# Zero fills of a decode kernel: DRAM as the source of zeros for the feed-forward stage and the end

## The chip, the cores and the metric

The kernel runs on one core of one Trainium2 chip. The metric is the device time of one execution in microseconds. The core has four computing engines, TensorE (PE), VectorE (DVE), ScalarE (ACT) and GpSimd (POOL), and SyncE (SP), which here only issues DMA transfers. All transfers, from whichever engine they are issued, run on the core's 16 DMA engines.

## The reference

The reference is the forward and backward pass of one decoder layer with adaptive layer norm, for a single token. It returns the output row and the gradients of ten inputs:

```python
mod = (silu(c) @ w_mod).reshape(1, 6, 1, 1024)      # sa, ca, ga, sb, cb, gb
h = layernorm(x) * (1 + ca) + sa
x = x + ga * attention(h, k_cache, v_cache, wq, wo)  # 32 heads, 4 KV heads, last 4096 of 65536 rows
h = layernorm(x) * (1 + cb) + sb
x = x + gb * ((sigmoid(h @ w_gate) * (h @ w_up)) @ w_down)   # 1024 -> 3584 -> 1024
out, vjp = jax.vjp(f, A_x, k_cache, v_cache, wq, wo, w_gate, w_up, w_down, c, w_mod)
return (out, *vjp(grad_out))
```

The attention reads only the last W = 4096 rows of each cache. The gradients of the two caches have the full shape [1, 4, 65536, 128], however, and all rows ahead of the last 4096 are zero. So 61,440 rows of 256 bytes are to be written with zeros for each of four KV heads and two caches: eight regions of 15 MB, 120 MB in all. (1 MB in this document's counts of fills is 1,048,576 bytes; the profile's MB are 1,000,000.)

## The kernel before, in words

**Stages.** The kernel loads the weights of the modulation, K and V, and wq (to about 50 us), computes scores and softmax, then for each KV head a product N of K, P and V (line 657), the fold of wo into the attention's gradient (`bch`, line 712, 64 steps), the modulation's remaining sections, the feed-forward stage in seven blocks of 512 columns (about 315 to 485 us), and an end in which the gradients of wo, w_mod, wq, K and V are formed and stored. The order of all work is written out by hand; the tile framework adds the waits between engines, and the schedule is not reordered.

**Fills.** The 120 MB of zeros are cut into 120 pieces of 1 MB. `zero(n, after)` issues the next n of them from POOL's queue; tables (`Z_Q`, `Z_SM`, `Z_N`, `Z_B`, `Z_GA`, `Z_CB`, `Z_FOLD`, `Z_FFN`, `Z_END`) say how many at each point of the program. `after` makes the fill wait for an earlier instruction, for pacing. A fill is one of three kinds:

- *Narrow* (7 pieces at positions 15, 45, 75, 93, 103, 113, 119 of the order): columns of the first region, as two DMAs (lines 173 and 176), 120 rows and a small remainder, from an SBUF tile `zeros`. The other rows' remainder is written once by `zero_rest`.
- *From SBUF* (line 186, 44 pieces): the tile `zeros` holds 128 partitions of 2048 one-byte zeros, and the DMA widens them to four bytes, so that each partition writes 8 KB. All fills outside the N and `bch` loops are of this kind, and those pieces of the first region that come up in them.
- *From DRAM* (line 180, 69 pieces): with `big=True`, which only the N loop and `bch` pass, the source is the first quarter of `zero_src`, a piece that has already been filled with zeros, widened in the same way. 32 rows of 32 KB are written.

```python
zero(Z_N[s], recent(mm, 6), True)       # N loop
zero(Z_B[nbq - 1 - len(bq)], recent(mm, 3), True)   # bch
zero(Z_GA)                              # all others: no third argument
```

The order of the pieces is `zero_src`, the eight wide pieces of the first region (128 rows at a stride of 122,880 bytes, 8 KB each), then the other seven regions, which are contiguous, with the narrow ones put in at their positions.

**Queues.** POOL's queue carries the fills, the loads of w_gate and w_up (`load_ug`, line 886, 512 KB each), the stores of their gradients (`store_ug`, line 890), and the stores of the end (lines 1164, 1169, 1205, 1212, 1216). POOL has eight DMA semaphores, used in turn, so that a DMA on it waits until the one eight before has landed. SP's queue carries w_down: `load_wd` (line 872) and `store_wd` (line 875), two halves of 512 KB for each block, in one buffer, so that the load of a half waits for the store of the same half. In each block VectorE's products with w_down (`wd_ttr`, line 227, and `wd_outer`, line 223) come after the matmuls `ffn_mm` (line 999), which wait for the load.

In each block q, `Z_FFN[q]` gives the fills at four places: after the first `store_ug`, after the second, after the last `wd_outer`, and after the second `load_ug` of block q + 2.

Of the kernel before, what the change touches and what calls it, by code (L numbers as in the profile page):

```python
# [10 lines left out]
P = 128  # L11
FP32 = mybir.dt.float32
BF16 = mybir.dt.bfloat16
FP8 = mybir.dt.float8e4
# [11 lines left out]
G = 4  # L26
# [11 lines left out]
NARROW = (15, 45, 75, 93, 103, 113, 119)  # L38

def spread(total, n):
    return [(i + 1) * total // n - i * total // n for i in range(n)]

NBP = 8
NT = 8
NGA = 9
# [5 lines left out]
Z_N = spread(31, 128)  # L53
Z_B = [n + (i in (31, 38)) for i, n in enumerate(spread(29, 43))] + [1, 1, 1, 1, 0] + [1, 0, 0, 1, 1, 1, 0, 0] + [1, 0, 1, 0, 1, 0, 0, 0]
# [4 lines left out]
def kernel(  # L59
# [26 lines left out]
    nc = tc.nc  # L86
    SKW = A_k_cache.shape[2] - W
# [16 lines left out]
    def vt(shape, name, dt=FP32):  # L104
        return pool.tile(shape, dt, name=name)
# [4 lines left out]
    ZW = 4096  # L110
    zeros = vt([P, ZW // 2], "zeros", FP8)
# [11 lines left out]
    def fill_rows(og, g):  # L123
        return og[0, g, 0:SKW, :].rearrange("r d -> (r d)")

    first_rows = fill_rows(out_2, 0).rearrange("(p x) -> p x", p=P)
    NZR = first_rows.shape[1] // ZW
    zregions = [first_rows[:, i * ZW:(i + 1) * ZW] for i in range(NZR)]
    flat = []
    for og in (out_2, out_3):  # L130
        for g in range(G):
            if og is not out_2 or g:
                whole = fill_rows(og, g).rearrange("(i x) -> i x", i=NZR)
                flat.extend(whole[i:i + 1, :] for i in range(NZR))

    zero_src = flat.pop(0)
    BIGP = 32

    def as_rows(piece, n):
        return piece.rearrange("i (p x) -> (i p) x", p=n)  # L140

    wide = [as_rows(zero_src, P)] + zregions[len(NARROW):] + flat
    narrow = zregions[0:len(NARROW)]
    zleft = []
    while narrow or wide:
        if narrow and (len(zleft) in NARROW or not wide):
            zleft.append((narrow.pop(0), True))
        else:
            zleft.append((wide.pop(0), False))
    nlen = len(NARROW)  # L150
    ncount = list(range(1, nlen + 1))
    NS = SKIP + 1
    rest = out_2[0, 0, 0:SKW, :].rearrange("r d -> (r d)").rearrange("(p x) -> p x", p=P)[0:8, 0:nlen * ZW].bitcast(FP32)
    assert nlen * 2 <= 20

    keep = [0]

    def dep(later, earlier):
        tc.add_manual_dep(later.ins, earlier.ins.name,
# [1 line left out]
                          reason="pace")  # L161

    def zero(n, after=None, big=False):
        for _ in range(n):
            if len(zleft) <= keep[0]:
                return
            region, narrow_ = zleft.pop(0)
            first = None
            if narrow_:  # L170
                nc.gpsimd.inc_swdge_sem([], [], mode="reset_dge_cursor")
                n = nlen - ncount.pop()
                first = nc.gpsimd.dma_start(
                    out=rest[0:NS, 0:nlen * 128].rearrange("p (t x) -> p t x", t=2)[:, :, n * 64:(n + 1) * 64],
                    in_=zeros[0:NS, 0:64].rearrange("p (t x) -> p t x", t=1).broadcast_to([NS, 2, 64]))
                ins = nc.gpsimd.dma_start(
                    out=region[8:P, :].bitcast(FP32).rearrange("(t p) x -> p t x", t=2),
                    in_=zeros[0:60, :].rearrange("p (t x) -> p t x", t=1).broadcast_to([60, 2, ZW // 2]))
            elif big and region.shape[0] == 1:
                ins = nc.gpsimd.dma_start(  # L180
                    out=as_rows(region, BIGP).bitcast(FP32),
                    in_=zero_src[:, 0:P * ZW // 4].rearrange("i (p x) -> (i p) x", p=BIGP).bitcast(FP8))
            else:
                if region.shape[0] == 1:
                    region = as_rows(region, P)
                ins = nc.gpsimd.dma_start(out=region.bitcast(FP32), in_=zeros[:, :])  # L186
            if after is not None:
                dep(first or ins, after)

# [19 lines left out]
    def tt(out, a, b, op):  # L209
        return nc.vector.tensor_tensor(out=out, in0=a, in1=b, op=op)  # L210
# [215 lines left out]
    for j in range(KD):  # L426
        for k in range(16):
            mm = nc.tensor.matmul(mod_ps[:, k:k + 1], lhsT=wm01_t[j][:, k * P:(k + 1) * P],
                                  rhs=cs_bf[:, j:j + 1], start=(j == 0 and k == 0), stop=(j == KD - 1),
                                  skip_group_check=True)  # L430
# [53 lines left out]
    for j in range(KD):  # L484
# [6 lines left out]
        for h in range(HQ):  # L491
            mm = nc.tensor.matmul(q_ps[:, h:h + 1], lhsT=wq_t[j][:, h * P:(h + 1) * P],  # L492
                                  rhs=h1_bf[:, j:j + 1], start=(j == 0 and h == 0), stop=(j == KD - 1),
                                  skip_group_check=True)
# [9 lines left out]
    for ch in range(8):  # L504
        ps = new_ps("sc_ps")
        for g in range(G):
            mm = nc.tensor.matmul(ps[32 * g:32 * g + 32, 0:512], lhsT=q_col2[:, HG * g:HG * g + 32],
                                  rhs=k_T[:, g, ch * 512:(ch + 1) * 512], start=True, stop=True,
                                  tile_position=(0, 32 * g))
# [132 lines left out]
    def recent(mm, lag):  # L642
        last_mm.append(mm)
        return last_mm[-lag] if len(last_mm) >= lag else last_mm[0]

    for g in range(G):
        nbank = bank_pair("n_ps", g)
        for t_ in range(KT):
            s = g * KT + t_
            vp = vp_t[(s // 2) % 2]  # L650
            if t_ % 2 == 0:
                tt(vp.rearrange("p t h d -> p (t h d)"),
                   v_nat[:, g, t_ * DH:(t_ + 2) * DH].rearrange("p (t o d) -> p t o d", t=2, o=1).broadcast_to([P, 2, HG, DH]),
                   pT2[:, g, HG * t_:HG * t_ + 2 * HG, :].rearrange("p n (o k) -> p n o k", o=1).broadcast_to([P, 2 * HG, 64, 2]),
                   ALU.mult)
            for k in range(2):
                mm = nc.tensor.matmul(nbank[k][:, :], lhsT=k_nat[:, g, t_ * DH:(t_ + 1) * DH],  # L657
                                      rhs=vp[:, t_ % 2, 4 * k:4 * k + 4, :].rearrange("p h d -> p (h d)"),
                                      start=(t_ == 0), stop=False)
            zero(Z_N[s], recent(mm, 6), True)  # L660
            if t_ == 20:
                build_bd(g)
            if s == 2:
                ok_cols(ok4)
            elif s == 4:
                ok_rows()
            elif s == 24:
                mod_gb((6, 7))
                load_wo(0)
            elif t_ % 2 == 1:  # L670
                side()
        for k in range(2):
            nc.tensor.matmul(nbank[k][:, :], lhsT=nkb_rows[:, :], rhs=bd[:, 4 * k:4 * k + 4, :].rearrange("p h d -> p (h d)"),
                             start=False, stop=True)
            c0 = (HG * g + 4 * k) * P
            nc.scalar.activation(out=N_sb[:, c0:c0 + 512], in_=nbank[k][:, :], func=ACT.Copy, scale=float(SCALE))
        load_wo(4 + g)
        if g < 3:
            jobs.extend(t_unit(h, "AA") for h in range(HG * g, HG * g + HG))
# [5 lines left out]
    bq = []  # L685
# [13 lines left out]
    nbq = len(bq)  # L699
    bbank = {}  # L700

    def bch(n=1):
        for _ in range(n):
            if not bq:
                return
            p, i, u = bq.pop(0)
            if i == 0:
                bbank[p] = bank_pair("b_ps", p)
            for a in range(4):
                h = 4 * u + a  # L710
                for k in range(2):
                    mm = nc.tensor.matmul(bbank[p][k][:, :], lhsT=a4[:, p, h, :], rhs=wo_t[u][:, a, k * 512:(k + 1) * 512],  # L712
                                          start=(i == 0 and a == 0), stop=(i == 7 and a == 3))
            zero(Z_B[nbq - 1 - len(bq)], recent(mm, 3), True)
            if i == 7:
                for k in range(2):
                    o = B_t[p][:, k * 512:(k + 1) * 512]
                    if k == 0 or p == NBP - 1:
                        nc.scalar.copy(out=o, in_=bbank[p][k][:, :])
                    else:  # L720
                        cp(o, bbank[p][k][:, :])
# [418 lines left out]
    dh1_ps = new_acc("dh1_ps")  # L1140
    for p in range(NBP):
        for it in range(KD):
# [95 lines left out]
    dh1 = vt([P, KD], "dh1")  # L1238
    cp(dh1[:, 0:NBP], dh1_ps[:, 0:NBP])
    dwo(4)  # L1240
# [34 lines left out]
    dx0b, _ = layernorm_bwd_col(dln1, ln1, rstd1, "ln1b")  # L1275
# [58 lines left out]
    for g in (2, 3):  # L1334
# [1 line left out]
        dwq_tile(4 + g, tail)  # L1336
        s2(2 * g, tail)
        s2(2 * g + 1, tail)
    keep[0] = 0
    zero(len(zleft))  # L1340
    assert not zleft and not narrow and not jobs and not bq

# [28 lines left out]
```

## Time and profile before

| What | Value |
|---|---|
| Median of 3 runs | 595.29 us (595.26 to 595.35) |
| The profiled execution's own time | 595.61 us |
| Its span in the profile | 593.8 us |
| Busy share of PE, DVE, ACT, POOL | 68%, 60%, 44%, 26% |
| DMA | 246.61 MB in 36,321 packets, mean 415 GB/s |
| Issues of fills: line 180 / 186 / narrow (173 and 176) | 69 / 44 / 7 and 7 |
| Median from issue to landing: lines 180 / 186 | 16.9 / 13.7 us |

The profile is of one execution. Its span runs from the first instruction of the program to the end of the last; the 1.8 us that its own time has beyond that lie outside. A DMA row's "us to landing" is the time from the issue to the completion, so it holds the time that the transfer stands in a queue. "DMA share" is the time that the packets took over 16 engines' time; it goes over 1 where the records of two packets of an engine overlap. In the waits, a row gives who waited for whom, the total in us, how many times, and the longest.

### The profile page before, as it was taken

What the parts mean: (1) busy time and instruction counts of PE and PEld (TensorE: products, weight loads), DVE (VectorE), ACT (ScalarE), POOL (GpSimd) and SP (SyncE); (2) the same over time, 40 slices, a digit from 0 to 9 for tenths busy, and PEclk for the clock granted to TensorE, in tenths of its full rate; (3) what the DMA queues carried; (4) which work ended last, traced back from release to release, by engine and by line L of the source; (5) the groups of instructions that cost most, each with busy time, mean ns of one, the idle gap of its engine ahead of it and who ended that gap; (6) DMA issues with size and microseconds to landing.
All of it is one profiled execution on the core that took longest, in us unless ns stands there. A gap on an engine that the chain in (4) does not pass through costs nothing.

```text
span 593.8 us, 10908 instructions
## 1 busy us (share of the span) xinstructions
PE 406.3 (68%) x4516; PEld 271.3 (46%) x4516; DVE 356.7 (60%) x674; ACT 263.6 (44%) x401; POOL 156.2 (26%) x255
## 2 busy tenths in 40 slices
PE   3997789999999989998876236344455294894410
PEld 3995434334344545544445225334344264593410
DVE  3754499999511010086628686596877885868650
ACT  2489514557211014213125366463665833893310
POOL 3113113212222112222221333223334252222200
PEclk9999699999999999999985566565555576855555
DMA  9999999999999999999999999999999999999997
GB/s 351 421 416 422 412 461 393 448 429 427 426 421 403 442 446 411 443 425 402 412 418 402 418 413 414 411 409 405 398 392 418 420 417 426 418 423 426 425 421 328
DMA packets 36321, 246.61 MB, mean 415 GB/s; under 512 B 5141, under 2 KB 5141, under 8 KB 22552
## 3 DMA queue, kind: packets, MB, share of 16 engines
q0 software_dynamic: 28976, 218.64, 91.8%
q1 hardware_dynamic: 7248, 27.27, 12.9%
q8 instruction: 35, 0.57, 0.4%
q14 instruction: 14, 0.11, 0.0%
q10 hardware_dynamic: 48, 0.01, 0.0%
HBM read 78.39 MB, written 185.60 MB: 445 GB/s over the span
## 4 chain that ended last, share of the span: by engine, by line
DMA 47%; PE 19%; DVE 17%; issue 6%; ACT 5%; POOL 1%; ACTq 0%; DVEq 0%; POOLq 0%; SPq 0%
DMA out_dram<-arena 16%; DMA out_dram<-out_dram 16%; PE n_ps L657 6%; DMA arena<-in_B_w_gate_dram 6%; DVE arena L227 5%; DVE arena L223 5%; DVE arena L210 4%; DMA arena<-in_B_w_down_dram 3%; DMA out_dram<-zeros 3%; DMA arena<-in_w_mod_dram 3%; ACT arena L476 2%; PE t_ps L619 2%; PE w_ps L415 1%; PE tp_k L455 1%; PE b_ps L712 1%
## 5 line engine op out<-in xcount | busy, mean ns | idle before, releaser
L712 PE MATMUL b_ps<-arena 128*128 128x512 bf16 x512 | 115.9, 379 | 1.1 <-ACT arena L858 1.1
L858 ACT COPY arena<-tp_side 128x1024 bf16<-128x1024 bf16 x62 | 60.9, 1014 | 70.3 <-PE tp_side L857 68.6
L210 DVE TENSOR_TENSOR arena<-arena 128x2048 bf16<-128x2048 bf16 x64 | 76.6, 1223 | 2.3 <-PE n_ps L657 0.3
L712 PEld LDWEIGHTS <-arena 128*128 128x128 bf16 x512 | 48.7, 98 | 57.6 <-issue 2.9
L227 DVE CUSTOM_DVE_ANT_0 arena<-arena,scr 128x1024 bf16<-128x1024 bf16 x56 | 66.3, 1222 | 9.8 <-ACT scr L1020 9.8
L657 PE MATMUL n_ps<-arena 128*128 128x512 bf16 x256 | 65.8, 378 | 6.2 <-DVE arena L210 4.6
L180 POOL DMA_DIRECT2D out_dram<-out_dram x69 | 34.1, 495 | 118.6 <-PE n_ps L657 36.0
L857 PE MATMUL tp_side<-ident_bf,arena 128*128 128x128 bf16 x496 | 55.5, 290 | 9.7 <-ACT arena L858 5.0
L857 PEld LDWEIGHTS <-arena 128*128 128x128 bf16 x496 | 47.3, 135 | 15.4 <-issue 8.5
L981 PE MATMUL fg<-h_bf,arena 128*128 128x1 bf16 x448 | 15.6, 166 | 44.3 <-DMA arena<-in_B_w_up_dram 26.2
L657 PEld LDWEIGHTS <-arena 128*128 128x128 bf16 x256 | 24.6, 97 | 41.6 <-issue 16.2
L227 DVE CUSTOM_DVE_ANT_0 arena<-arena,b1k 128x1024 bf16<-128x1024 bf16 x24 | 28.4, 1221 | 19.5 <-PE fg L999 19.5
L186 POOL DMA_DIRECT2D out_dram<-zeros x44 | 24.8, 565 | 56.8 <-PE q_ps L492 16.1
L258 ACT ACTIVATE arena<-scr,h 128x1024 bf16<-128x1024 bf16 x35 | 38.5, 1142 | 2.3 <-DVE dh2acc L227 1.8
L890 POOL DMA_DIRECT2D out_dram<-arena x28 | 22.1, 795 | 65.8 <-ACT arena L258 46.5
L1200 ACT ACTIVATE arena<-ps_kv 128x512 bf16<-128x512 f32 x48 | 26.2, 687 | 23.1 <-PE ps_kv L1196 22.9
L621 ACT CAST arena<-t_ps 128x512 bf16<-128x512 f32 x56 | 30.1, 589 | 12.1 <-PE t_ps L619 12.1
L981 PEld LDWEIGHTS <-arena 128*128 128x128 bf16 x448 | 13.9, 105 | 46.9 <-DMA arena<-in_B_w_up_dram 27.7
L219 DVE CAST arena<-b_ps 128x512 bf16<-128x512 f32 x6 | 4.2, 692 | 51.1 <-PE b_ps L712 51.1
L1196 PE MATMUL ps_kv<-junk,arena 8*128 8x128 bf16 x256 | 27.3, 305 | 8.7 <-DVE arena L223 7.6
L1196 PEld LDWEIGHTS <-arena 8*128 8x128 bf16 x256 | 25.3, 141 | 10.5 <-issue 10.5
L476 ACT COPY arena<-tp_wq 128x1024 bf16<-128x1024 bf16 x23 | 21.7, 1044 | 7.8 <-PE tp_wq L474 7.7
(310 smaller groups left out, 648.1 us busy)
## 6 DMA issues: line engine op xcount, KB each, us to landing
out_dram<-zeros POOLq DMA_DIRECT2D x44, 1024.0 KB, 13.7
out_dram<-arena POOLq DMA_DIRECT2D x28, 1024.0 KB, 17.4
out_dram<-arena POOLq DMA_DIRECT2D x30, 512.0 KB, 11.0
out_dram<-arena SPq DMA_DIRECT2D x20, 512.0 KB, 9.8
arena<-in_A_wq_dram POOLq DMA_DIRECT2D x8, 1024.0 KB, 20.6
arena<-in_A_wo_dram POOLq DMA_DIRECT2D x8, 1024.0 KB, 13.2
arena<-in_w_mod_dram POOLq DMA_DIRECT2D x7, 1024.0 KB, 18.0
arena<-in_B_w_up_dram POOLq DMA_DIRECT2D x14, 512.0 KB, 11.6
```

The costliest lines, as they stand in the source:

```text
L180: ins = nc.gpsimd.dma_start(out=as_rows(region, BIGP).bitcast(FP32), in_=zero_src[:, 0:P * ZW // 4].rearrange("i (p x) -> (i p) x", p=BIGP ...
L210: return nc.vector.tensor_tensor(out=out, in0=a, in1=b, op=op)
L223: return nc.vector.tensor_scalar(out=out, in0=a, scalar1=s1, scalar2=None, op0=op0)
L227: return nc.vector.tensor_tensor_reduce(out=out, in0=w, in1=b, scale=1.0, scalar=0.0, op0=ALU.mult, op1=ALU.add, accum_out=acc)
L258: return nc.scalar.activation(out=out, in_=b, func=ACT.Copy, scale=col)
L476: nc.scalar.copy(out=blk, in_=tp[:, :])
L621: nc.scalar.copy(out=o, in_=ps)
L657: mm = nc.tensor.matmul(nbank[k][:, :], lhsT=k_nat[:, g, t_ * DH:(t_ + 1) * DH], rhs=vp[:, t_ % 2, 4 * k:4 * k + 4, :].rearrange("p h d -> ...
L712: mm = nc.tensor.matmul(bbank[p][k][:, :], lhsT=a4[:, p, h, :], rhs=wo_t[u][:, a, k * 512:(k + 1) * 512], start=(i == 0 and a == 0), stop= ...
L857: nc.tensor.transpose(tp[:, i * P:(i + 1) * P], blk[:, i * P:(i + 1) * P], ident_bf[:, :])
L858: nc.scalar.copy(out=blk if dst is None else dst, in_=tp[:, :])
L1196: nc.tensor.matmul(ps[:, t4 * DH:(t4 + 1) * DH], lhsT=rows[32 * g:32 * g + HG, t_ * P:(t_ + 1) * P], rhs=hd[32 * g:32 * g + HG, :], start= ...
```

## The change

The kind of a fill no longer depends on who calls `zero` but on its position. The first eight pieces are written from the SBUF tile, as before (`"chip"`). All other pieces that are not narrow are written from the first quarter of `zero_src` in DRAM, as 16 rows of 64 KB (`"long"`); the pieces of the first region, too, which now are 16 of its 128 rows over all columns that the narrow fills leave, and which stand at the end of the order instead of near its front. `TRIPLE` would let a region be cut into pieces of 3 MB; with ones throughout it has no effect, and each fill stays 1 MB. The number of fills at each place, the narrow ones' positions and the pacing stay.

```diff
+NCHIP = 8
+TRIPLE = (1, 1, 1, 1, 1, 1, 1)
...
-    wide = [as_rows(zero_src, P)] + zregions[len(NARROW):] + flat
-    narrow = zregions[0:len(NARROW)]
+    narrow = [first_rows[:, i * ZW:(i + 1) * ZW] for i in range(nlen)]
+    single = []
+    triple = []
+    for i, (og, g) in enumerate([(out_2, 1), (out_2, 2), (out_2, 3), (out_3, 0), (out_3, 1), (out_3, 2), (out_3, 3)]):
+        mine = fill_rows(og, g).rearrange("(i x) -> i x", i=NZR // TRIPLE[i])
+        (single if TRIPLE[i] == 1 else triple).extend(mine[k:k + 1, :] for k in range(mine.shape[0]))
+    zero_src = single[0]
+    single.extend(first_rows[16 * k:16 * k + 16, nlen * ZW:] for k in range(8))
...
+    while narrow or single or triple:
+        if narrow and at in NARROW:
+            zleft.append((narrow.pop(0), "narrow", 1))
+        elif triple and at >= NCHIP and at + 3 <= next(i for i in NARROW if i >= at):
+            zleft.append((triple.pop(0), "long", 3))
         else:
-            zleft.append((wide.pop(0), False))
+            zleft.append((single.pop(0), "chip" if at < NCHIP else "long", 1))
+        at += zleft[-1][2]
...
-    def zero(n, after=None, big=False):
-        for _ in range(n):
-            if len(zleft) <= keep[0]:
-                return
-            region, narrow_ = zleft.pop(0)
+    def zero(n, after=None):
+        credit[0] += n
+        while zleft and credit[0] >= zleft[0][2]:
+            region, kind, size = zleft.pop(0)
+            credit[0] -= size
...
-            elif big and region.shape[0] == 1:
+            elif kind == "chip":
+                ins = nc.gpsimd.dma_start(out=region.rearrange("i (p x) -> (i p) x", p=P).bitcast(FP32), in_=zeros[:, :])
+            else:
+                rows = 16 * size
+                if region.shape[0] == 1:
+                    region = region.rearrange("i (p x) -> (i p) x", p=rows)
                 ins = nc.gpsimd.dma_start(
-                    out=as_rows(region, BIGP).bitcast(FP32),
-                    in_=zero_src[:, 0:P * ZW // 4].rearrange("i (p x) -> (i p) x", p=BIGP).bitcast(FP8))
-            else:
-                if region.shape[0] == 1:
-                    region = as_rows(region, P)
-                ins = nc.gpsimd.dma_start(out=region.bitcast(FP32), in_=zeros[:, :])
+                    out=region.bitcast(FP32),
+                    in_=zero_src[:, 0:rows * 8192].rearrange("i (p x) -> (i p) x", p=rows).bitcast(FP8))
...
-            zero(Z_N[s], recent(mm, 6), True)
+            zero(Z_N[s], recent(mm, 6))
...
-            zero(Z_B[nbq - 1 - len(bq)], recent(mm, 3), True)
+            zero(Z_B[nbq - 1 - len(bq)], recent(mm, 3))
...
-    keep[0] = 0
-    zero(len(zleft))
+    zero(sum(size for _, _, size in zleft))
```

More of the change, by code (lines that the diff above doesn't have):

```diff
@@ L126 @@
     first_rows = fill_rows(out_2, 0).rearrange("(p x) -> p x", p=P)
+    nlen = len(NARROW)
     NZR = first_rows.shape[1] // ZW
[L128 to L140, printed above, removed]
-    wide = [as_rows(zero_src, P)] + zregions[len(NARROW):] + flat
-    narrow = zregions[0:len(NARROW)]
-    zleft = []
-    while narrow or wide:
-        if narrow and (len(zleft) in NARROW or not wide):
-            zleft.append((narrow.pop(0), True))
-        else:
-            zleft.append((wide.pop(0), False))
-    nlen = len(NARROW)
+    assert NZR - nlen == 8 and NZR % 3 == 0
+    narrow = [first_rows[:, i * ZW:(i + 1) * ZW] for i in range(nlen)]
[6 more added lines that the diff above has]
+    single.extend(first_rows[16 * k:16 * k + 16, nlen * ZW:] for k in range(8))
+    zleft = []
+    at = 0
+    while narrow or single or triple:
[3 more added lines that the diff above has]
+            zleft.append((triple.pop(0), "long", 3))
+        else:
+            zleft.append((single.pop(0), "chip" if at < NCHIP else "long", 1))
+        at += zleft[-1][2]
+    assert not narrow and not triple and at == NZR * 8
     ncount = list(range(1, nlen + 1))
     NS = SKIP + 1
-    rest = out_2[0, 0, 0:SKW, :].rearrange("r d -> (r d)").rearrange("(p x) -> p x", p=P)[0:8, 0:nlen * ZW].bitcast(FP32)
+    rest = first_rows[0:8, 0:nlen * ZW].bitcast(FP32)
     assert nlen * 2 <= 20
-    keep = [0]
+    credit = [0]
     def dep(later, earlier):
@@ L161, in dep @@
                           reason="pace")
-    def zero(n, after=None, big=False):
-        for _ in range(n):
-            if len(zleft) <= keep[0]:
-                return
-            region, narrow_ = zleft.pop(0)
+    def zero(n, after=None):
[3 more added lines that the diff above has]
+            credit[0] -= size
             first = None
-            if narrow_:
+            if kind == "narrow":
                 nc.gpsimd.inc_swdge_sem([], [], mode="reset_dge_cursor")
```

## The prediction

> **What bounds the kernel now.** I read the page first: its DMA lines, then the chain that ended last.
>
> ```profile
> DMA  9999999999999999999999999999999999999997
> DMA packets 36321, 246.61 MB, mean 415 GB/s; under 512 B 5141, under 2 KB 5141, under 8 KB 22552
> ...
> q0 software_dynamic: 28976, 218.64, 91.8%
> q1 hardware_dynamic: 7248, 27.27, 12.9%
> ...
> HBM read 78.39 MB, written 185.60 MB: 445 GB/s over the span
> ...
> DMA 47%; PE 19%; DVE 17%; issue 6%; ACT 5%; POOL 1%; ACTq 0%; DVEq 0%; POOLq 0%; SPq 0%
> ```
>
> The 16 DMA engines are busy in every slice, while VectorE, the next busiest apart from TensorE's pipelined matmuls, works 60% of the span, and DMA is the largest part of the chain (47%). So the time is close to bytes over rate: 246.61 MB at 415 GB/s is 594 us. No bytes are removed by the change on the written side (44 + 69 fills of 1 MB remain), so what counts is how fast a fill passes, and whether the engines ever run dry.
>
> Next the stage table, over stretches in which nearly nothing but one kind of fill is in the engines. The columns are the stretch, its length, the busy time of PE, PEld, DVE, ACT and POOL, the clock, the DMA share and GB/s.
>
> ```profile
> 71.50:81.50 10.00, 8.30 (x69) 3.82 (x58) 7.73 (x19) 2.88 (x10) 1.55 (x3) 1.00 1.15 427
> 187.00:194.00 7.00, 7.00 (x62) 3.49 (x59) 1.38 (x2) 2.45 (x3) 2.10 (x4) 1.00 1.12 415
> 487.00:495.00 8.00, 7.07 (x147) 6.93 (x144) 4.54 (x16) 7.61 (x12) 3.34 (x6) 0.75 1.14 423
> 210.50:235.00 24.50, 22.36 (x227) 13.37 (x225) 4.22 (x21) 7.88 (x11) 5.50 (x10) 1.00 1.02 429
> 316.00:484.00 168.00, 76.13 (x1142) 65.19 (x1143) 126.87 (x279) 95.98 (x107) 57.70 (x83) 0.54 1.11 410
> ```
>
> The first three are fills from SBUF (8-KB packets), the fourth is fills from DRAM, the last is the feed-forward stage, where most of the fills to be changed lie. The DMA rows of the fourth stretch say what a DRAM fill is: 320 packets and 10.49 MB, half of the packets under 512 B, so 160 packets of 65,536 B, 16 to a fill. So 64-KB packets pass at 429 GB/s and 8-KB packets at 415 to 427.
>
> Last, who waits in the feed-forward stage, and how long a DMA of SP's takes there.
>
> ```profile
> PE fg L999 <- DMA arena<-in_B_w_down_dram: 19.6, 7, 5.8
> ...
> DVE arena L227 <- PE fg L999: 19.5, 7, 4.3
> ...
> out_dram<-arena SPq DMA_DIRECT2D x14, 512.0 KB, 9.8
> arena<-in_B_w_down_dram SPq DMA_DIRECT2D x12, 512.0 KB, 9.7
> ```
>
> VectorE stands 19.5 us for matmuls that stand for the w_down loads. The arithmetic, then, hangs on SP's transfers, although the engines are full: both are tight in this stage.
>
> **The change part by part.** *69 fills of the attention stage* (L180 now) go from 32 rows of 32 KB to 16 rows of 64 KB. They are 16 packets of 64 KB already, so I cost this at nothing; the fourth rival holds the case that it is not.
>
> *36 fills* go from the SBUF source to the DRAM source: of the 44 issues at L186, the first 8 stay. By issue times they are 1 at 74 us, 3 at 177 to 182, 1 at 267, 2 at 302 and 310, 28 in 316 to 484 us, and 1 at 495. Each goes from 128 packets to 16, so the packets fall by 36 x 112 = 4032. The time of one fill is 1,048,576 B over the rate. The three SBUF stretches, weighted by length, give 422 GB/s: 2.482 us. The DRAM stretch gives 2.444 us. The difference, 0.038 us, times 36 is 1.4 us. The table counts a packet where it starts, and a round of 64-KB packets at an edge moves its rate; cut half a microsecond or a microsecond otherwise, that stretch gives 424 to 432. When each packet's bytes are instead shared out over its own duration, the rates are about 424.5 and 430, which gives 0.032 us a fill and 1.1 us. The bounds are the worst and best pairs of rows: 424 against 427 is a loss of 0.6 us, 432 against 415 a gain of 3.6 us. I take 1.2 us, between the two ways of counting. As the engines are full around all 36, all of it lies on the path.
>
> *Reading zeros* adds 36 x 0.262 MB = 9.4 MB of reads to HBM. Within the DRAM fills' 2.444 us this is already paid, as they read the same quarter. The Trainium skill, "HBM Reference", Specifications, gives about 358 GB/s of HBM bandwidth as one core's share (and says that a core alone measures more); were that share the limit, 9.4 MB would cost an estimated 26 us by the page. This trace does not agree that it is: it moves 445 GB/s over the span, and the DRAM stretch writes 429 and reads a quarter of that besides.
>
> *POOL* issues a DRAM fill in 488 ns (median at L180) against 555 ns (L186): 36 x 0.067 = 2.4 us less on an engine that is busy for 26% of the span. Nothing, as the DMA queue in front of it hides it. No wait is added: the pacing dependences are kept; the one new reading fill, at 74 us, reads a piece that was issued at 48.4 us and whose like land in 7.3 to 19.5 us. The eight pieces of the first region move from the front of the order to its end, beside narrow fills that use other columns of the same rows. Should a wait be put between these, POOL would hold one fill's landing (13.7 us median), with L1169's and L1164's stores behind it; the 12 to 19 us from issue to landing around 480 to 512 us cover all or most of one.
>
> *SP's transfers* are the cost that this trace shows only at one place. From 284 to 316 us SP loads w_down and w_mod while DRAM fills are in the engines:
>
> ```profile
> arena<-in_B_w_down_dram SPq DMA_DIRECT2D x1, 512.0 KB, 13.2
> ```
>
> That is 3.4 us over the 9.8 of the later ones. A 64-KB packet holds an engine for 2.4 us, eight times as long as an 8-KB packet. The Trainium skill, "DMA: Bandwidth & Descriptors", Queues, rings and completion order, says that an engine alternates between its queues at packet boundaries; the one row above agrees with that, and no other row here tests it. Below, a buffer half of w_down goes round as store (9.8), load (9.8) and 3.9 us from landing to the next store: 23.5 us, and the stores come every 23.85 us (315.7 to 458.8 in six rounds). So there is next to no slack in this loop. It ends the program later only by what makes the engines run dry. Against that stands POOL's queue: its stores in this stage land 10.9 us after issue (median), the first load of the trace with nothing ahead of it after 3.7, so about 7.2 us of work stands ahead (4.4 where it is thinnest, 8.1 to landing). I cost it at nothing in the sum, because fills that SP waits behind are work done, and keep the price for the rival. From below: with POOL's own loads served sooner beside a slower SP, the two dips of the feed-forward stage (slices of 4.2 us at 359, 374 and 352 GB/s against 415) could close, which is worth 160/415 x 4.2 = 1.6 us.
>
> **Sum.** The profiled execution took 595.61 us, of which 593.8 is the span. 595.61 - 1.2 = 594.4. The median of the runs, 595.29, is 0.32 lower, which gives 594.1.
>
> **The rivals.** *Engines stay full, fills pass 1.2 us faster in all* (the forecast, 594.1, own range 593.0 to 595.0). For it: the DMA row, and no GB/s slice of the page falls under 390 between the first and last. Against: the gain is 0.3% of the DMA time and hangs on 2% between two rates.
>
> *The dips close too.* 594.1 - 1.6 = 592.5. For it: at the dips POOL's loads are waiting on stores to land (POOL L886 waits 14.7 us in this stage on them). Against: SP's slower loop pulls the other way.
>
> *SP's w_down loop falls behind* (the other side). Place: store and load of each half in the five rounds with a load. Price: if each round becomes longer by one 64-KB packet, 5 x 2.44 = 12.2 us, less 7.2 us that POOL's queue covers: 5.0 us, so 594.1 + 5 = 599 at that price, 598 with some of it falling where the queue is deeper. The bounds are 0, and 5 x 2 x 3.4 - 7.2 = 27 us if every transfer took 13.2. It decides from the point where the rounds have lost more than the 4.4 to 7.2 us of queue. For it: the 13.2 us row and VectorE's 19.5 us. Against: when the queue is thin there are fewer fills to stand behind (the store at 412.6 us, into a thin queue, landed in 7.6), so the loop mends itself.
>
> *HBM is the limit after all.* 9.4 MB at the measured 445 GB/s is 21 us: 615. Against: the DRAM stretch is the fastest of the table.
>
> *The pieces are not 64 KB.* If rows of 64 KB were cut to 8 KB, the gain would be gone and the 69 would lose 69 x 0.038 = 2.6 us: 597.9. Against: the same 16 runs of 64 KB appear already.
>
> **How the numbers follow.** Chances: forecast 0.60, dips close 0.13, SP's loop 0.22, HBM 0.02, pieces 0.03. A measurement of this kernel tells 0.2% from no change, that is under 594.1 or over 596.5. The forecast lies on the first line; I put 0.28 of it below and 0.32 in between. Faster: 0.28 + 0.13 = 0.41. Same: 0.32 + 0.02 of SP's loop, where its price is under 2 us, = 0.34. Slower: 0.20 + 0.02 + 0.03 = 0.25. The range goes from 592.5 to 599.0; outside lie some 0.05 below, and about 0.10 of SP's loop and HBM above.
>
> **What would show it.** Right: about 32,290 packets, 88 MB read from HBM, 105 issues at the DRAM line and 8 from zeros, the feed-forward stage at 412 to 413 GB/s, and the DMA row at 9 throughout. The loop's rival shows as w_down landing over 11 us, a longer wait of PE fg on it, and DMA slices under 350 GB/s. Wrong is the forecast if the time moves by more than 2 us with the DMA row unbroken: then a 64-KB packet has another price beside SP's packets and POOL's 4-KB ones than alone.

## The result, and the profile after

| Kernel | Runs | Median (lowest to highest) |
|---|---|---|
| before | 20 | 595.62 us (595.26 to 596.55) |
| after | 20 | 596.46 us (595.88 to 597.64) |

The ratio is 1.0015, with a 95% interval of 1.0009 to 1.0021: slower by some 0.9 us. That is within the range of the prediction, but on the other side of no change than the forecast. The profiled execution took 596.67 us, 1.06 more than that of before.

The page of after, the lines that answer to those of before:

```profile
DMA  8999999999999999999999999999999999999997
GB/s 353 418 418 419 415 458 396 452 420 437 428 424 429 416 440 400 439 425 420 403 424 434 399 386 356 388 415 445 385 407 434 429 439 388 421 421 429 423 423 331
DMA packets 32289, 246.61 MB, mean 415 GB/s; under 512 B 5141, under 2 KB 5141, under 8 KB 22552
...
q0 software_dynamic: 24944, 218.64, 89.9%
q1 hardware_dynamic: 7248, 27.27, 11.8%
...
HBM read 87.82 MB, written 185.60 MB: 460 GB/s over the span
...
PE 37%; DMA 25%; DVE 22%; ACT 6%; issue 6%; POOL 0%; ACTq 0%; DVEq 0%; SPq 0%; POOLq 0%
...
L186 POOL DMA_DIRECT2D out_dram<-out_dram x105 | 52.9, 505 | 145.6 <-PE n_ps L659 45.1
```

The change does what it says: 4032 packets fewer, 9.43 MB more read from HBM, 105 issues with DRAM as the source. DMA's share of the chain has fallen from 47% to 25%, but that isn't the loss: E5 below, which is faster than before, has 26%, and the largest part of PE's 37% (12%) lies in the `bch` loop, where the rate is that of before (431 GB/s against 429 from 210.5 to 235 us). One place stands out in the GB/s row, the slices 386, 356 and 388, at 342 to 387 us, in the feed-forward stage. (From line 210 of before on, the same line is 2 higher in after and 14 higher in E3, E4 and E8.)

The stretches there, first of before, then of after (columns as in the prediction: busy time of PE, PEld, DVE, ACT, POOL; the clock; the DMA share; GB/s):

```profile
330.00:350.00 20.00, 6.63 (x84) 5.78 (x84) 13.92 (x30) 10.02 (x11) 7.43 (x11) 0.59 1.07 414
350.00:360.00 10.00, 4.84 (x91) 4.52 (x92) 5.64 (x14) 4.30 (x7) 4.30 (x6) 0.50 1.13 414
360.00:370.00 10.00, 6.19 (x79) 5.39 (x76) 8.37 (x18) 6.53 (x7) 3.58 (x5) 0.59 1.10 415
...
410.00:450.00 40.00, 16.94 (x236) 14.82 (x236) 33.07 (x69) 23.52 (x25) 15.08 (x21) 0.50 1.07 396
```

```profile
330.00:350.00 20.00, 4.58 (x67) 4.16 (x68) 8.38 (x20) 3.89 (x5) 7.42 (x11) 0.53 1.00 395
350.00:360.00 10.00, 5.45 (x102) 4.82 (x101) 9.15 (x18) 9.54 (x12) 1.71 (x2) 0.61 0.92 345
360.00:370.00 10.00, 6.11 (x77) 5.17 (x76) 8.57 (x20) 5.26 (x7) 6.12 (x9) 0.54 1.06 364
...
410.00:450.00 40.00, 17.42 (x248) 15.04 (x248) 32.14 (x66) 23.88 (x26) 13.90 (x20) 0.50 1.06 416
```

Between 330 and 370 us after falls behind, and from 410 to 450 it gets part back, since the two dips of before are gone. To add this up I shared out each packet's bytes over its own duration, which a large packet at an edge doesn't disturb. Up to 370 us, before has moved 155.00 MB and after 153.63: 1.37 MB, at 415 GB/s 3.3 us lost. From 370 to 450, after moves 0.70 MB more than before (1.7 us back), and from 450 to 580 another 0.15 MB (0.4 us). The sum, 1.2 us lost, is close to the 1.06 of the two executions. (Before and E11 run the same program up to 370 us and differ by 0.16 MB at 310, so a part of 0.15 MB says nothing by itself.)

**What is late at 350 us.** The feed-forward stage's waits and DMA rows of after:

```profile
PE fg L1001 <- DMA arena<-in_B_w_down_dram: 28.3, 9, 8.2
DVE arena L229 <- PE fg L1001: 23.7, 7, 6.8
```

```profile
out_dram<-arena SPq DMA_DIRECT2D x13, 512.0 KB, 12.1
arena<-in_B_w_down_dram SPq DMA_DIRECT2D x12, 512.0 KB, 9.8
```

TensorE stood 19.6 us for w_down before, now 28.3. The median load is as before (9.8 against 9.7); the median store has gone from 9.8 to 12.1. So it is the store that has become slower, and each load waits for the store out of the same buffer half. The first round shows it best. SP issued two stores between 312 and 322 us. The rows give the landing of the first (no landing is recorded for the second), before and then after:

```profile
out_dram<-arena SPq DMA_DIRECT2D x2, 512.0 KB, 10.6
```

```profile
out_dram<-arena SPq DMA_DIRECT2D x2, 512.0 KB, 14.9
```

By the packets' records, the second of these (issued at 319.2 in before, 319.0 in after) has its last packet written 8.95 us after issue in before, and 13.83 in after. Its neighbours are the fills that POOL issued at 309.6, 315.8, 319.3 and 319.8, which now are 64-KB packets. Followed from there: the load into its half is issued at 330.15 in before and 334.18 in after, its last packet comes 8.08 and 10.27 later, the matmuls wait for it, and VectorE for them. So 4.0 us come from the store and another 2.2 from the load, together 6.2, by which VectorE's first product with that half is late (before, then after):

```profile
339.40 1.21 DVE L227 CUSTOM_DVE_ANT_0 arena<-arena,b1k 128x1024 bf16<-128x1024 bf16 x1
```

```profile
345.61 1.23 DVE L229 CUSTOM_DVE_ANT_0 arena<-arena,b1k 128x1024 bf16<-128x1024 bf16 x1 [3.79 <-PE fg L1001]
```

VectorE's products release ScalarE's, and these the stores that POOL issues next. POOL's timeline around it, of before and then of after (start, length, and in brackets the idle time ahead and its releaser):

```profile
344.78 0.67 POOL L176 DMA_DIRECT2D out_dram<-zeros  x1 [0.30 <-DMA out_dram<-zeros]
351.39 1.71 POOL L890 DMA_DIRECT2D out_dram<-arena  x2 [5.95 <-ACT arena L258]
```

```profile
344.44 0.67 POOL L177 DMA_DIRECT2D out_dram<-zeros  x1 [0.27 <-DMA out_dram<-out_dram]
357.69 1.71 POOL L892 DMA_DIRECT2D out_dram<-arena  x2 [12.59 <-ACT arena L260]
```

POOL issues nothing for 12.6 us, and what it had queued lasts until about 356.5. Then the engines run dry, which three short stretches of after show:

```profile
356.50:359.50 3.00, 0.00 (x0) 0.00 (x0) 2.94 (x7) 3.00 (x6) 1.71 (x2) 0.50 0.75 261
360.00:362.50 2.50, 1.08 (x21) 0.83 (x19) 2.19 (x7) 1.39 (x2) 0.30 (x1) 0.50 0.97 251
365.00:367.50 2.50, 2.25 (x22) 2.09 (x21) 2.50 (x5) 1.60 (x2) 1.48 (x2) 0.50 1.07 308
```

In the first the DMA share is 0.75: too little work. In the other two the engines are occupied and pass little all the same: the 4-KB packets last 254 and 235 ns on average, against 164 and 167 in the same stretches of before. No 64-KB packet is in the engines then: the last one ahead starts at 352.7 us, the next at 367.5.

### The profile page after: what moved, and what is told of

The parts are those of the page before. It is cut to its first block, busy times and chain, and to the rows that moved or that the text cites. A ratio compares the mean times of both kernels' runs of the same rounds, so it can differ in the third digit from the quotient of the medians.

```text
span 594.9 us, 10884 instructions
## 1 busy us (share of the span) xinstructions
PE 403.4 (68%) x4492; PEld 269.9 (45%) x4516; DVE 356.9 (60%) x674; ACT 263.4 (44%) x401; POOL 155.1 (26%) x255
## 2 busy tenths in 40 slices
DMA packets 32289, 246.61 MB, mean 415 GB/s; under 512 B 5141, under 2 KB 5141, under 8 KB 22552
## 3 DMA queue, kind: packets, MB, share of 16 engines
q1 hardware_dynamic: 7248, 27.27, 11.8%
HBM read 87.82 MB, written 185.60 MB: 460 GB/s over the span
## 4 chain that ended last, share of the span: by engine, by line
PE 37%; DMA 25%; DVE 22%; ACT 6%; issue 6%; POOL 0%; ACTq 0%; DVEq 0%; SPq 0%; POOLq 0%
PE b_ps L714 12%; DMA out_dram<-arena 9%; DVE arena L212 6%; PE n_ps L659 6%; DVE arena L229 5%; DVE arena L225 5%; DMA arena<-in_B_w_gate_dram 4%; DMA arena<-in_B_w_down_dram 4%; DMA out_dram<-out_dram 3%; DMA arena<-in_w_mod_dram 3%; PE t_ps L621 2%; DMA out_dram<-zeros 2%; PE tp_side L859 2%; PE tp_wq L476 2%; PE w_ps L417 2%
## 5 line engine op out<-in xcount | busy, mean ns | idle before, releaser
L714 PE MATMUL b_ps<-arena 128*128 128x512 bf16 x495 | 113.8, 379 | 2.1 <-ACT arena L860 1.1
L186 POOL DMA_DIRECT2D out_dram<-out_dram x105 | 52.9, 505 | 145.6 <-PE n_ps L659 45.1
L623 ACT CAST arena<-t_ps 128x512 bf16<-128x512 f32 x56 | 30.1, 589 | 12.1 <-PE t_ps L621 12.1
L1198 PE MATMUL ps_kv<-junk,arena 8*128 8x128 bf16 x256 | 27.1, 304 | 10.1 <-DVE arena L225 8.8
L983 PEld LDWEIGHTS <-arena 128*128 128x128 bf16 x448 | 13.8, 104 | 37.8 <-DMA arena<-in_B_w_up_dram 19.5
L1001 PE MATMUL fg<-hh_bf,arena 128*128 128x1 bf16 x224 | 8.1, 166 | 30.8 <-DMA arena<-in_B_w_down_dram 28.3
```

The lines of the kernel that those rows point to most:

```text
L623: nc.scalar.copy(out=o, in_=ps)
L983: nc.tensor.matmul(gu[:, col:col + 1], lhsT=ug_v[:, q % 2, j // 4, j % 4, k, f0:f0 + 255:2], rhs=h2_bf[:, j:j + 1], start=(j == 0 and i == ...
L1198: nc.tensor.matmul(ps[:, t4 * DH:(t4 + 1) * DH], lhsT=rows[32 * g:32 * g + HG, t_ * P:(t_ + 1) * P], rhs=hd[32 * g:32 * g + HG, :], start= ...
```

## The experiments

The theory is that the 64-KB fills ahead of the first feed-forward block hold up SP's second store, and with it the loop of store and load. Against it stand, among others, that 64-KB packets anywhere in the stage are the cause, and that the reads of zeros cost HBM time; the expectations give each its numbers. All kernels with their times, against before on the same chip (E1 to E4 on one chip, E5 to E8 on another, E9 to E12 on a third; 11 or 12 runs each, before 33 to 35, median 595.53 to 595.58). The other columns are each of one profiled execution. "Store" is the time from the issue of the 319-us store to its last packet's end, "restart" the issue of the next `store_ug` (351.39 before, 357.69 after), and the last two columns are GB/s with bytes shared out (before 415 and 414, after 367 and 338).

| Kernel | Median us | Ratio (95%) | Store | Restart | 350-360 | 360-370 |
|---|---|---|---|---|---|---|
| E1 fold fills from SBUF | 594.82 | 0.9993 (0.9982-1.0004) | 9.61 | 351.37 | 417 | 418 |
| E2 before + 64 KB in the fold | 595.80 | 1.0005 (0.9996-1.0014) | 14.07 | 356.60 | 389 | 396 |
| E3 DRAM, 8 KB | 595.68 | 1.0002 (0.9993-1.0011) | 10.13 | 351.39 | 415 | 415 |
| E4 DRAM, 16 KB | 595.16 | 0.9995 (0.9986-1.0004) | 10.49 | 351.97 | 417 | 417 |
| E8 DRAM, 32 KB | 596.43 | 1.0014 (1.0005-1.0023) | 13.36 | 357.59 | 365 | 344 |
| E5 after + second buffer | 594.79 | 0.9988 (0.9980-0.9997) | 11.81 | 351.29 | 416 | 413 |
| E6 before + second buffer | 596.03 | 1.0008 (0.9999-1.0017) | 8.20 | 349.90 | 411 | 413 |
| E7 block 0 from SBUF | 596.36 | 1.0019 (1.0006-1.0032) | 13.96 | 358.33 | 377 | 341 |
| E9 block 1 from SBUF | 595.64 | 1.0003 (0.9995-1.0012) | 13.93 | 357.38 | 363 | 384 |
| E10 E1 + two fills moved | 594.63 | 0.9984 (0.9975-0.9993) | 9.84 | 351.38 | 417 | 418 |
| E11 before + two fills moved | 595.58 | 1.0007 (0.9996-1.0017) | 9.84 | 352.22 | 416 | 416 |
| E12 no fills at 319 us | 596.18 | 1.0013 (1.0004-1.0022) | 9.77 | 349.11 | 421 | 416 |

The restart and the two rates go together: where POOL starts again by 352.3 us there is no dip at 350, where it starts after 356 there is one.

**E1 and E2: the fold's fills alone.** E1 takes five pieces (positions 85 to 89, issued from 302 to 320 us) back to SBUF; E2 is before with those five from DRAM.

```diff
-            zleft.append((single.pop(0), "chip" if at < NCHIP else "long", 1))
+            zleft.append((single.pop(0), "chip" if at < NCHIP or 85 <= at < 90 else "long", 1))
```

```diff
-    zero(Z_FOLD[0])
+    zero(Z_FOLD[0], None, True)
```

(and so for the other three of `Z_FOLD`.)

> The changed kernel, but the five fills just ahead of and in the first feed-forward block (positions 85 to 89, issued at 300 to 320 us) come from SBUF in 8-KB packets again. Theory A (64-KB packets hold up SP's w_down store and load in the first block, and the engines run dry at 350 to 370 us): the slices at 350 and 360 us (367 and 338 GB/s in the changed kernel) come back to over 400, SP's second store of the first block has its last packet 9 us after issue instead of 13.8, and the time falls by some 3 us to 593 to 594, under the kernel before. Theory B (64-KB fills are dearer everywhere among the 4-KB transfers of the feed-forward stage): 5 of some 33 fills change, so 0.1 to 0.2 us of the 0.9 comes back, 596.3. Theory C (the loss comes from reading zeros from HBM, whatever the packets): as B.

> The kernel before, with only the same five fills read from DRAM in 64-KB packets. Theory A: the loss without the gain, a dip at 350 to 370 us, 595.6 + 3 = 598 to 599. Theories B and C: 595.7 to 595.8, and no dip there.

E1 took back the loss (its interval lies below that of after, 1.0009 to 1.0021): POOL's stores come again at their old time.

```profile
351.37 1.71 POOL L892 DMA_DIRECT2D out_dram<-arena  x2 [6.11 <-ACT arena L260]
```

But the time, 594.82, falls short of what was expected: with the work no longer late, the dips at 410 to 420 and 440 to 450 are back (388 and 391). E2 has most of the delay (store 14.07, restart 5.2 us late for after's 6.3) from five pieces, so the place is right.

```profile
356.60 1.71 POOL L890 DMA_DIRECT2D out_dram<-arena  x2 [11.44 <-ACT arena L258]
```

Its time alone, 595.80, is what theories B and C gave; it is the dip (389 and 396), which they excluded, that speaks for A. The price was expected too high: up to 370 us E2 is 0.66 MB, 1.6 us, behind before, and then the later dips close (411 and 400 for 375 and 389), so that 0.3 us are left by the medians, which the interval doesn't tell from nothing. The two together say that the fold's fills make the delay. The dip is less deep in E2 than in after; why, is open.

**E3, E4 and E8: the source and the length apart.** From position 85 on, the fills read zeros from DRAM as after does, but in 128 rows of 8 KB, 64 of 16 KB or 32 of 32 KB. (Regions are cut at a stride, so that a row is no longer than that.)

```diff
+    ROWS = 128        # 64, 32
...
+    single[90:105] = [part[:, i * P * ZW // ROWS:(i + 1) * P * ZW // ROWS] for i in range(NZR)]
...
+            elif kind == "rows":
+                ins = nc.gpsimd.dma_start(
+                    out=region.bitcast(FP32),
+                    in_=zero_src[:, 0:P * ZW // 4].rearrange("i (p x) -> (i p) x", p=ROWS).bitcast(FP8))
```

> The changed kernel, but from position 85 on each fill writes 128 rows of 8 KB at a stride, with zeros still read from DRAM, so packets are 8 KB and the source is DRAM. Theory A: SP alternates with short packets, no dip at 350 to 370 us, and the time is that of before or a little less, 595.0 to 595.7. Theory B: as A. Theory C (the reads cost): as slow as the changed kernel or slower, 596.5 or more.

> As the run before, with 64 rows of 16 KB. Theory A: SP waits for packets of 0.6 us instead of 0.3; little or no dip at 350 to 370 us, 594.5 to 595.5, as half of the gain in rate of the long packets is there. Theory B: between the 8-KB run and the changed kernel, 595.5 to 596. Theory C: 596.5 or more.

> The changed kernel, with 32 rows of 32 KB from position 85 on, two packets an engine. Theory A: SP waits behind packets of 1.2 us; the dip at 350 to 370 us is between those of 16 KB (none) and 64 KB (3.6 us): some 1 us; 595.3 to 596. Theory B: also between, 595.8.

E3 reads as much from HBM as after, and its feed-forward stage stands where that of before stood (410):

```profile
HBM read 87.82 MB, written 185.60 MB: 460 GB/s over the span
```

```profile
316.00:484.00 168.00, 76.29 (x1134) 65.14 (x1135) 126.22 (x279) 95.97 (x107) 57.00 (x83) 0.53 1.11 411
```

So the reads cost nothing that these runs could tell (E3's interval goes from -0.4 to +0.7 us). What counts is the length of a packet, and not in proportion: the store takes 8.95 us beside 8 KB from SBUF, 10.13 and 10.49 beside 8 and 16 KB from DRAM, then 13.36 beside 32 KB, nearly the 13.83 beside 64. (E11, which is before up to that point, has 9.84, so a difference under 1 us says nothing.) For E8 I had expected something in between, and got the whole loss:

```profile
357.59 1.71 POOL L904 DMA_DIRECT2D out_dram<-arena  x2 [12.47 <-ACT arena L272]
```

The Trainium skill, "DMA: Bandwidth & Descriptors", Queues, rings and completion order, says that an engine goes round its queues and drains a whole packet from one before it turns to the next. The traces agree that longer packets of one queue delay the other; a delay that is in full at half the length is more than that sentence tells, and whether what the page calls a packet is the profile's packet, no run shows.

**E5 and E6: the loop cut.** Here w_down gets a second buffer, used in turn by blocks, so that the load of a block needn't wait for the last block's store; output 9 is computed from other data in both, as the second buffer takes its place.

```diff
-    wd_v = ar(152, 8).rearrange("p (i d) -> p i d", i=4)
+    wd_two = [ar(152, 8).rearrange("p (i d) -> p i d", i=4), ar(48, 8).rearrange("p (i d) -> p i d", i=4)]
...
-        nc.sync.dma_start(out=wd_v[:, 2 * s:2 * s + 2, :], in_=wd_dram(B_w_down, q, s))
+        nc.sync.dma_start(out=wd_two[q % 2][:, 2 * s:2 * s + 2, :], in_=wd_dram(B_w_down, q, s))
```

> The changed kernel with a second buffer for w_down (blocks alternate), so that a w_down load waits for no store of the block before. The buffer lies where pieces of w_mod were kept for one product at the end, so output 9 is computed from other data; the instructions are the same. Theory A (the loss is the first block's store, then load, in one buffer, behind 64-KB packets): w_down lands long before it is needed, the slices at 350 and 360 us come back over 400 GB/s, and the kernel is 1 to 3 us faster than the changed one, 593.5 to 595. Theory B (64-KB packets slow the 4-KB transfers of the stage as such): the loss against the next run stays, near 0.9 us.

> The kernel before with the same second buffer (output 9 computed from other data). It says what the buffer alone is worth. Theory A: the run before this one is faster than this one by the gain of the 36 fills, 0.7 to 1.2 us. Theory B: it is slower by 0.9 us.

The fills are those of after, all of them, and the dip is gone. The waits of E5 in the stage:

```profile
PE fg L1001 <- DMA arena<-in_B_w_down_dram: 12.1, 6, 6.8
DVE arena L229 <- PE fg L1001: 18.4, 6, 5.4
```

TensorE's wait for w_down falls from 28.3 to 12.1. E5's store still takes 3.6 us longer than E6's (11.81 against 8.20), and there is no dip. So the slower store hurts through the buffer that the load needs. E5 against E6 is the change with the loop out of the way: 594.79 - 596.03 = -1.24 us. That is the forecast's gain (1.2), but so close by luck: E6 is 0.45 us over before for the buffer alone, E5 is 0.79 under it, and the two intervals leave room for -0.1 to -2.2. Theory B's loss of 0.9 us is excluded.

**E7 and E9: which 64-KB fills count.** E7 is after with the three pieces at positions 90 to 92 from SBUF, E9 with those at 94 and 95, which are issued at 363.7 and 364.2 us, right after the dry spell. The edit is that of E1 with other positions.

> The changed kernel, but the three fills issued in the first feed-forward block (positions 90 to 92, at 333 and 343 us) come from SBUF; the five ahead of them stay long. Theory A: the store of the first block is still late (last packet 14 us after issue), its load and the second block's store less so, so the dip at 350 to 370 us is as small as in the run with only five long fills (1.4 us) and the later fills' gain stays: 594.8 to 595.3. Theory B: 3 of some 33 fills, 596.3.

> The changed kernel, but the two fills issued right after the dry spell (positions 94 and 95, at 363.7 and 364.2 us) come from SBUF. The run with only five long fills had a milder dip at 360 us (396 GB/s) than the changed kernel (338) and the run with the first block's three from SBUF (341). Theory A1 (the dip's depth comes from 64-KB packets that follow at once on the dry spell, when all engines run in step): the slice at 360 us comes back to 390 or more, 595.0 to 595.6. Theory A2 (the depth comes from the length of the delay alone): the slice stays near 340, 596.4.

E7 is a miss: the dip stays (its execution runs 1.4 us later than that of after from ahead of the store on, and so do the times in its row). Its 596.36 is theory B's number; but B is excluded by E5 against E6. By the time these three are issued (two at 333.3), the store at 319 is already late, so the delay comes from the fold's own fills. E9 leaves the dry spell where it was (363 GB/s from 350 to 360 us) and moves more behind it: 384 against 338, and the 4-KB packets at 360 to 362.5 us last 189 ns for after's 254. But the exchanged fills can't be the reason for that: in E9 their first packet starts at 366.4 us, in after at 367.5, and E2 and E7 have 188 and 191 ns at 360 to 362.5 too. Of the 0.46 MB that E9 moves more from 360 to 370 us, 0.16 are moved before 366.4. E9's time, 595.64, is 0.8 us under after by medians, near what theory A1 gave, but on another chip, and the intervals overlap (0.9995 to 1.0012, 1.0009 to 1.0021). So it isn't shown that 64-KB packets behind a dry spell cost anything.

**E10, E11 and E12: where the fills stand.** E10 is E1, E11 is before, each with a fill more in blocks 3 and 4 of the seven (counted from 0) and two fewer in the last. E12 is after with the two fills at 319 us moved to these blocks.

```diff
-Z_FFN = [(0, 2, 0, 2), (0, 2, 0, 1), (0, 2, 0, 2)] + [(0, 1, 0, 2)] * 2 + [(1, 1, 1, 3), (1, 2, 1, 0)]
+Z_FFN = [(0, 2, 0, 2), (0, 2, 0, 1), (0, 2, 0, 2)] + [(0, 2, 0, 2), (0, 2, 0, 2), (1, 1, 1, 3), (0, 2, 0, 0)]
```

```diff
-Z_FOLD = (1, 1, 1, 2)
+Z_FOLD = (1, 1, 1, 0)
```

> The run with the five fills from SBUF (594.8), and besides one fill more after the second store of w_gate and w_up in the fourth and in the fifth block, taken from the last block. The dips at 410 to 420 and 439 to 443 us (1.5 us in all) are there when POOL has too little issued. If that is their cause they close, and the kernel takes 593.1 to 593.6; if they come from the loads and stores themselves, 594.8.

> The kernel before with the same two fills moved: 595.6 - 1.5 = 594.1 if the dips close, 595.6 if not. Beside the run before this one it says whether the 64-KB packets' gain and the move add up.

> The changed kernel, all fills long, but the two fills issued at 319 us beside SP's second store are moved to the fourth and the fifth block. Theory A: SP's store has its last packet by 11 us after issue, the dip at 350 to 370 us is gone or under 1 us, those at 410 and 440 us are closed, 593.2 to 594.2. If the engines run dry at 325 to 335 us for the want of the two fills, 595 or more.

E12 says what the two fills at 319 are there for, and comes out as the second half of its expectation. Without them the store is quick (9.77), there is no dip at 350, and the engines are dry 30 us earlier instead:

```profile
320.00:330.00 10.00, 5.86 (x97) 5.08 (x95) 9.55 (x18) 9.63 (x13) 1.57 (x2) 0.50 0.77 291
```

```profile
326.90 1.57 POOL L892 DMA_DIRECT2D out_dram<-arena  x2 [10.54 <-ACT arena L260]
```

They are cover for the 10.5 us in which POOL has nothing to issue. With 64-KB packets the same two are cover and hindrance.

E10 is the fastest of all, 594.63, and faster than before by more than the noise (0.9984, 0.9975 to 0.9993); that the moved fills add to E1 is not shown (594.82). But the moved fills closed both dips in E10 and E11 (411 GB/s or more in each 10 us from 410 to 450) and brought 0.2 us and nothing; I had expected some 1.5. At 450 us E10 is 0.65 MB ahead of E1, at 490 0.40, at 580 still 0.27. Part of the lead goes in the block that gave up the two fills: from 480 to 488 us E10 has 396 GB/s, E1 416. The last part of the chain that ended last, of E1 and then of E10 (start and length):

```profile
489.76 18.48 DMA out_dram<-arena
508.78 19.17 DMA out_dram<-arena
530.48 2.44 DVE arena L225 x2
```

```profile
494.20 13.98 DMA out_dram<-arena
508.73 19.32 DMA out_dram<-arena
530.57 2.45 DVE arena L225 x2
```

From 508.7 us on the two agree to 0.1 us, although E10 has less left to write. What holds that point fixed was not tried.

## Why the prediction was wrong

**The step that failed** is that of SP's transfers: "I cost it at nothing in the sum, because fills that SP waits behind are work done". They are work done, but the work is then used up when the arithmetic behind SP is late. The prediction had the mechanism, the place and the deciding point as a rival, with a chance of 0.22, and the point was worked out from landings that it gave: the loop decides when it has lost more than 4.4 to 7.2 us of POOL's queue. Measured: the store 4.9 us later at its last packet, the load that waits for it issued 4.0 later and 2.2 slower itself, the restart of POOL's stores 6.3 us later (357.69 - 351.39). The cover was 5.1 us (the engines ran out at 356.5, the next stores of before are issued at 351.39). The 13.2-us row from 284 to 316 us, which counted for the rival only, looks like the same thing, fills of 64 KB beside a transfer of SP's; no run varied those. The medians that I went by (10.9 us of POOL's queue, 9.8 of the store) are those of a whole stage; it was decided at one place, where four fills stood together.

**The rival's size** was off in another way. It had five rounds falling behind by 2.44 us each. In fact the first lost it at once, and the later ones mended themselves, as the "against" said. Its 5.0 us became 3.3. (A 64-KB packet lasts 2.44 us and an 8-KB one 0.33 to 0.35, so seven times as long, not eight.)

**The dips** of before closed too, and after moved 0.70 MB (1.7 us) more there, where 1.6 us was worked out. That was a rival of its own, with a chance of its own; it came true in one kernel with SP's loop, as its consequence: what is late by 3 us falls into the stretch in which before had too little to move. Taking the two as excluding each other was a mistake: -1.2 (fills) + 3.3 - 1.7 is +0.4, against +1.06 in the profile and +0.84 in the medians; the 3.3 and the 1.7 hold a part of the fills' gain already, which the account by bytes doesn't separate. Nor is a closed dip time gained as such: E11 has both closed, is 0.54 MB ahead of before at 450 us, and takes as long.

**What held.** The fills are faster where the loop is out of the way: 1.2 predicted, 1.24 between E6 and E5, 0.8 between before and E5, 0.7 between before and E1, which has 31 of the 36 long and an interval that reaches no change. The reads for nothing measurable (E3, with 460 GB/s over the span). The Trainium skill, "HBM Reference", Specifications, gives about 358 GB/s as a core's share; the trace does not agree that this bounds the one core that runs here. 32,290 packets, 88 MB, 105 and 8 issues: 32,289, 87.82, 105 and 8. The 69 pieces of the attention stage: the stretch from 210.5 to 235 us, 429 GB/s before, has 431.

**What didn't show as said.** The feed-forward stage at 412 to 413 GB/s is at 406. "w_down landing over 11 us" as the rival's sign: the loads are at 9.8 in the median, as before; the stores show it, and so does the longer wait of PE fg (28.3 us). The DMA row of the page stays at 9 from the second slice on, as for an unbroken queue; a slice of 14.9 us is too coarse for a dry spell of 3 us, and the GB/s row beneath it (356) is the one that shows it.

## What to carry to other kernels

In this kernel the length of the fillers' packets set how long another queue's short transfers stood behind them. Ahead of such a change, look for the loop in which a transfer's end frees a buffer, and compare its delay with the queue's cover at the tightest place, not by the stage's medians. Fillers beside such a loop can stay short where the others become long: E1 and E10 do so with five short ones, and E10 is faster than before by 0.9 us.

## What was not expected of the hardware

The delay of the store is a step and not a line: 8.2 to 9.8 us beside 8-KB packets from SBUF, 10.1 beside 8-KB and 10.5 beside 16-KB ones from DRAM, 13.4 beside 32, 13.8 to 14.1 beside 64 (11.8 in E5, where the load no longer waits for it). The 16- and 32-KB values are of one execution each. And engines that had just been dry pass 4-KB packets slowly while they count as busy (235 to 254 ns for 164, a DMA share of 0.97 at 251 GB/s). At 360 to 362.5 us they last 188 to 254 ns in the five kernels that are late there (after, E2, E7, E8, E9) and 164 to 167 in the others. E12 has the same behind its own dry spell, 263 ns at 330 to 332 us, where only 4-KB and 4-byte packets pass. So no long packet has to be in the engines at the time; what makes them slow is open.
